# Loading q, k and v as float16 through GpSimd's queue in an attention + Fourier-mixing + FFN kernel

## The chip, the cores and the metric

The kernel runs on one NeuronCore of a Trainium2 chip. A core has TensorE (PE; its weight loads are shown as PEld), VectorE (DVE), ScalarE (ACT), GpSimd (POOL) and SyncE (SP), and 16 DMA engines, which carry what SP, ACT and POOL issue. DMAs issued from SP and ACT are on hardware queues (q1 and q10 in the profile), those from GpSimd on the software queue (q0). The metric is the time of one execution on the device in microseconds, and the median of the runs counts.

## The reference

Inputs are q, k, v of shape (batch 4, heads 8, sequence 768, head size 64), `n_global` 8, `n_local` 96, and two weights w_ch1 (512 x 2048) and w_ch2 (2048 x 512), all float32.

```python
scores = q @ k^T / 8 + bias            # bias = -slope[head] * distance
scores = where(key < 8 or 0 <= row - key < 96, scores, -1e9)
a = softmax(scores)
x = (a @ v)                            # (4, 768, 512), heads side by side
mixed = real(fft(fft(x, axis=1), axis=2))
u = x + mixed
un = (u - mean(u)) / sqrt(var(u) + 1e-6)
out = u + maximum(un @ w_ch1, 0) @ w_ch2
```

## The kernel before

Batches b = 0 to 3 go through attention and mixing one after the other; heads go in pairs, hp = 0 to 3, and n = 4 b + hp numbers the pairs. A batch's 768 rows become three groups of 256 rows for the FFN, c = 3 b + pr, 12 in all.

**Attention.** For each pair, q and k are transposed to head size x sequence (`trans`, tile `qkT`). For b < 2 TensorE does it: 48 transposes of 64x64 into the PSUM tile `pt` (L583), which L594 (DVE) or L598 (ACT) copies out. For b = 2 and 3, SP issues DMA transposes, three a pair (L557, L560). `score` makes the banded scores in three parts g; for b < 2 TensorE also adds the bias (L629, L641) and ScalarE's exponential (L665) writes `ex`; for b >= 2 the exponential goes to `er` (L662) and VectorE multiplies a mask in (L677). `kg_copies` (L544, GpSimd) gathers the 8 global keys; `v_global` and `glob` do the global part, whose exponential is `eg` (L741). `av` multiplies with v (L765, L776) and VectorE divides by the sums (L795, L796), which gives x.

**Mixing.** `bounce` writes x to DRAM and reads it back in another row order (tile `xr`). `fold_s` and `fold_d` (VectorE, some on ScalarE) fold x for the FFT along the sequence, `y_unit` multiplies with a table (L987), `mirror` (GpSimd, L1022 to L1035) reverses columns, `u_unit` does the second FFT (`pu`, L1067), adds x (L1086, L1095), and makes `un` (L1117, L1119). For c < 6 TensorE transposes `un` (`ptu`, L1158), for the others a DMA does. GpSimd makes the inverse deviation (L1133, L1134).

**FFN.** `ph` (L1188) is the first product, for which the first weight must be there; ScalarE or VectorE applies the relu (L1194, L1195). `pg` (L1212, from c = 8 on `pgA` and `pgD`, L1293) is the second product. No `ph` is emitted before the early PSUM banks C and D are given back (token `CD`), that is, before all of b = 0 through `u_unit` and the scores of b = 1.

**Loads.** SP loads q, k and v as float32 into staging tiles, which borrow the space of `hT`, `qs`, `u`, `w1` and `w2` (L407; for v of b >= 2 two half loads, L378). Casts follow: q and k on ACT (L411), DVE (L413) or GpSimd (L415) into the tile `qk`; v for b < 2 on GpSimd (L456) and then through TensorE into its place by products with the identity (`v_place`, L472, with idle products at L465) and out of PSUM by L490 (DVE) and L491 (ACT); v for b >= 2 on GpSimd straight into its place (L501). The weights are loaded and cast by GpSimd's DMAs, eight of 512 KB in float16 (L1472, L1477), after q and k of b = 1. Loads of b = 2 stand behind a small DMA on SP that waits for the last weight (`hold`, L1486, token `gate`).

**Order.** The order of every engine's instructions is written when the program is built, by the class `Plan`. It keeps a clock for each engine, assumes a cost for each instruction and emits what it thinks can start first; `BIAS` moves single ones. Each engine then runs its own list in order, GpSimd's and SP's lists including the DMA issues, and an instruction whose input is late holds those behind it.

Of the kernel before, what the change touches and what calls it, by code (L numbers as in the profile page):

```python
# [22 lines left out]
class Plan:  # L23
# [8 lines left out]
    LAND = {("xw", 0, 0): 34.0, ("xw", 0, 1): 36.0, ("xr", 0): 41.0, ("ld", 4, 2): 47.7, ("ld", 5, 2): 53.4, ("ld", 6, 2): 58.9, ("ld", 7, 2): 64.7, ("w1", 0): 44.6, ("w1", 1): 48.2, ("w1", 2): 52.2, ("w1", 3): 55.8, ("w2", 0): 59.5, ("w2", 1): 63.6, ("w2", 2): 66.6, ("w2", 3): 69.1}  # L32
    LAT = {"ACT": 0.14, "DVE": 0.12, "POOL": 0.08}

    def __init__(self):
        self.t = {"PE": 0.0, "ACT": 0.0, "DVE": 0.0, "POOL": 0.0, "SP": 0.7, "DMA": 1.9, "DMA2": 0.0}
        self.tok = {}
        self.ready = []
        self.pending = []
        self.rings = {}  # L40
        self.left = {}
        self.n = 0
        self.lanes = [0.0] * 8

# [23 lines left out]
    def later(self, ways, needs=(), after=0.0, outs=(), uses=(), ring=None, lat=0.0, dma=0.0, then=None, rank=1, nd=None):  # L68

        self.n += 1  # L70
        if nd is None:
            nd = int(dma > 0 and ways[0][0] in ("SP", "ACT"))
        self.pending.append((self.n, ways, list(needs), after, outs, uses, ring, lat, dma, then, rank, nd))
        self.promote()
# [11 lines left out]
    def first(self):  # L86

        best = None
        for i, (ready, p) in enumerate(self.ready):
            if p[11]:  # L90
                ready = [max(r, self.lanes[p[11] - 1]) for r in ready]
            c = (min(max(self.t[w[0]], r) for w, r in zip(p[1], ready)) - self.AHEAD * (p[10] < 0) + self.BIAS.get(p[4][0] if p[4] else None, 0.0),
# [4 lines left out]

    def emit(self, place):
        ready, (_, ways, needs, after, outs, uses, ring, lat, dma, then, _, nd) = self.ready.pop(place)
        if nd:  # L100
            ready = [max(r, self.lanes[nd - 1]) for r in ready]
# [14 lines left out]
        for _ in range(nd):  # L116
            self.lanes.append(max(end + lat, self.t[eng] + 2.2, *[self.LAND.get(o, 0.0) for o in outs]))
            self.lanes.pop(0)
# [4 lines left out]
        self.promote()  # L123

# [9 lines left out]
    def slot(self, tag):  # L134
# [7 lines left out]
    BIAS = {(1, 5): -0.7, ('ss', 1, 1): -3, (2, 27): -0.7, ('ex', 1, 3, 2): -3, (1, 46): -0.7, ('qk', 10, 1): -1.5, ('c', 't1'): 1.5, ('w1', 2): 3,  # L142
            ('er', 4): -0.7, ('ss', 2, 0): 0.7, ('h', 6, 6): 3, ('qk', 5, 0): 3, ('qkT', 6): -0.7, ('c', 't2'): 0.3, ('ex', 1, 2, 0): -0.7,
            ('xb', 11, 2): -1.5, ('h', 6, 5): 3, ('ss', 2, 1): 0.7, ('qkT', 10): -0.7, ('ex', 0, 2, 1): -1.5, (3, 13): 0.7, (1, 42): 0.7,
            ('un', 7, 0): -0.7, ('s', 11, 3): 0.7, ('x', 0, 3, 2): -1.5, ('qk', 9, 0): 1.5, ('qk', 7, 1): -0.7, ('qk', 0, 0): 1.5,
            ('ld', 15, 1): 1.5, ('h', 5, 1): 0.3, ('h', 5, 4): 0.3, ('qk', 11, 1): 0.7, (3, 73): -1.5, ('un', 0, 1): -1.5, ('y', 1, 2, 0): 3,
            ('er', 2): 0.3, ('qkT', 8): 0.7, ('h', 8, 4): -1.5, ('w1', 0): 3, ('vc', 2): 0.7, (1, 36): 0.3, (3, 47): 0.3, ('ld', 8, 1): -1.5,
            ('ob', 11, 1): -3, ('qkT', 14): 0.7, ('er', 19): -0.3, ('h', 8, 0): -1.5, (1, 92): -0.7, ('kG', 14, 0): 0.3, ('u', 5, 0): 0.3,
            ('w2t', 0): 0.3, ('z', 3, 0): 3, (1, 64): -1.5, ('v', 0, 2, 0): -0.3, ('ss', 6, 1): 3, (2, 21): -1.5, (2, 19): 0.3, ('rd', 10, 0): -0.7,
            ('sid', 2): -0.3, (3, 51): -3, (2, 5): -3}  # L150
    AHEAD = 0.0

    def run(self, streams):

        left = [[(*u, (i, k)) for k, u in enumerate(s)] for i, (s, _) in enumerate(streams)]
        while True:
            best = None
            for i, s in enumerate(left):
                for k, (needs, ring, _, name) in enumerate(s[:self.LOOK if streams[i][1] else 1]):
# [13 lines left out]
                    c = (max(r, self.t["PE"]) + self.BIAS.get(name, 0.0), i, k, g or "", max(r, self.t["PE"]))  # L173
# [37 lines left out]
def kernel(  # L211
# [105 lines left out]
    NBUF = {"hT": 3, "qk": 2, "qs": 3, "qkT": 4, "er": 2, "v0": 2, "eg": 1, "x": 1, "xr": 1, "zy": 1, "eA": 1,  # L317
# [25 lines left out]
    v16 = [kon.tile([P, NS, H, 66], FP16, tag=f"v16{i}", name=f"v16{i}") for i in range(2)]  # L343
# [14 lines left out]
    def vat(n):  # L358

        return ("u", min(n, HP)) if n < HP or n == 2 * HP - 1 else ("qs", 2 + n - HP)  # L360

    def load(b, hp, which):
        n = HP * b + hp
        h0 = 2 * hp
        gate = [("gate",)] if n == FB * HP else []
        if b >= FB:
            srcs = [(0, q), (1, k)] if which == "qk" else [(2, v)]
            for w, src in srcs:
                i = 1 + HP + 3 * (n - FB * HP) + w

                def run(src=src, i=i, w=w):
                    t = stage[("t", n, w)] = buf("qs", i, [P, 2 * NS, Dh], FP32, 1)
                    if w < 2:
                        run_dma(t.rearrange("p (m t) d -> p m (t d)", t=2), src, b, h0)
                        return
                    x = src[b, h0:h0 + 2].rearrange("h s d -> (h s) d").rearrange("(n m t) d -> t m n d", m=64, t=2)
                    for t2 in range(2):
                        nc.sync.dma_start(t[64 * t2:64 * t2 + 64], x[t2])  # L378
                pl.later([("SP", 0.55 if w < 2 else 1.1, run)], free("qs", i) + gate, 0.0, [("ld", n, w)], lat=1.7, dma=1.5 if w < 2 else 2.5, nd=1 + (w > 1))
                if w < 2:  # L380
                    cast_direct(b, hp, w, i)
        elif which == "v":
            def run():
                t = stage[("t", n, 2)] = buf(*vat(n), [P, NS, 2 * Dh], FP32, 1)
                run_dma(t, v, b, h0)
            pl.later([("SP", 0.55, run)], free(*vat(n)) + [("xi",)] * (n >= HP), 0.0, [("ld", n, 2)], lat=1.7, dma=1.45)
        else:
            tag, ti, users, slot = (("hT", hp, 2, 0) if hp < 3 else ("qs", 0, 1, None)) if b == 0 else \
                (("w1", "w2")[hp // 2], 0, 4, 2 * (hp % 2))
            for w, src in enumerate((q, k)):  # L390
                at = (tag, ti) if slot is not None else (tag, w)

                def run(w=w, src=src, at=at):
                    if slot is None:
                        t = buf(at[0], at[1], [P, NS, 2 * Dh], FP32, 1)
                    else:
                        if at not in stage:
                            stage[at] = buf(at[0], at[1], [P, users, NS, 2 * Dh], FP32, users)
                        t = stage[at][:, slot + w]
                    stage[("t", n, w)] = t  # L400
                    run_dma(t, src, b, h0)
                pl.later([("SP", 0.55, run)], free(*at), 0.0, [("ld", n, w)], lat=1.7, dma=1.45)
                cast_qk(b, hp, w, at)

    def run_dma(t, src, b, h0):

        nc.sync.dma_start(t, src[b, h0:h0 + 2].rearrange("h s d -> (h s) d").rearrange("(m p t) d -> p m (t d)", p=P, t=2))  # L407

    def copy_on(on, d, s):
        if on == "ACT":  # L410
            A(d, s, AF.Copy)  # L411
        elif on == "DVE":
            V.tensor_copy(d, s)  # L413
        else:
# [1187 lines left out]
```

The softmax here doesn't subtract the row's maximum and nothing guards it: scores larger than these inputs give would overflow.

## Time and profile before

| | |
|---|---|
| median of 3 runs | 263.72 us (263.44 to 265.83) |
| profiled execution: its time, which is its span | 263.7 us |
| PE, DVE, ACT, POOL busy | 246.5, 173.3, 151.4, 67.2 us |
| packets on q1 (SP), share of the 16 DMA engines | 69,298, 57.3% |
| packets on q0 (GpSimd: the weights), share | 4,224, 9.8% |
| first `ph` product | 53.1 us |
| read from HBM | 31.59 MB |

The page cuts the span into 40 slices of 6.6 us and gives each engine's busy share in tenths. The chain that ended last is followed back from the last instruction, at each step to what released it. A group of instructions is named by its line, engine, operation and tiles. A DMA share of 1.00 means that the packets' times add up to all of the 16 engines' time; it can pass 1, as packets of different queues overlap.

### The profile page before, as it was taken

Reading aid. Unit: us, or ns where it says so; the run is one execution under the profiler, and the core shown is the slowest. Engines: PE = TensorE matmul, PEld = TensorE weight load, DVE = VectorE, ACT = ScalarE, POOL = GpSimd, SP = SyncE. Lnnn points to the kernel's source line nnn. Section 1 sums busy time; section 2 is a strip of 40 time slices with the busy share of each in tenths; the row PEclk is TensorE's granted clock in tenths of the full one; section 3 lists DMA queues with packets and bytes.
Section 4 is the critical chain, followed back from the end, with each engine's and each line's share of the span. In section 5 each row is a group of like instructions: output and inputs, shape, how many; then the busy total and the mean of one; then the engine's idle time right before and its main releaser. Section 6 shows DMA issues by size and latency. Waiting matters only on the chain.

```text
span 263.7 us, 7306 instructions
## 1 busy us (share of the span) xinstructions
PE 246.5 (93%) x3080; PEld 180.6 (68%) x3080; DVE 173.3 (66%) x355; ACT 151.4 (57%) x257; POOL 67.2 (25%) x130
## 2 busy tenths in 40 slices
PE   8678778799999999999999999999999999999993
PEld 2556555578765785776685465677678778888883
DVE  3348999853399536782578958578995935644373
ACT  3276999756647655795682364993544265433300
POOL 1334335980041063514101623011221311000000
PEclk9799999979999999999999999999999999999998
DMA  7999959999699998999999897303641440310222
GB/s 211 296 293 272 309 142 289 225 196 201 125 223 172 283 267 106 183 212 157 218 160 207 205 281 116 90 2 82 145 137 40 23 114 25 83 40 2 80 80 82
DMA packets 76386, 42.02 MB, mean 159 GB/s; under 512 B 33474, under 2 KB 72514, under 8 KB 76354
## 3 DMA queue, kind: packets, MB, share of 16 engines
q1 hardware_dynamic: 69298, 32.65, 57.3%
q0 software_dynamic: 4224, 4.19, 9.8%
q10 hardware_dynamic: 2832, 4.72, 6.8%
q8 instruction: 24, 0.39, 0.6%
q14 instruction: 8, 0.07, 0.1%
HBM read 31.59 MB, written 9.44 MB: 156 GB/s over the span
## 4 chain that ended last, share of the span: by engine, by line
PE 77%; ACT 10%; DVE 5%; DMA 2%; issue 1%; POOL 1%; SPq 1%; DVEq 0%
PE ph L1188 30%; PE pg L1212 21%; PE pgD L1293 5%; ACT ex L665 4%; PE pgA L1293 4%; PE pav L776 4%; PE pu L1067 3%; PE py L987 3%; DMA u<-in_v_dram 2%; PE sc L638 2%; DVE qkT L594 2%; ACT er L662 2%; PE pav L765 1%; ACT un L1117 1%; POOL ww L1035 1%
## 5 line engine op out<-in xcount | busy, mean ns | idle before, releaser
L1188 PE MATMUL ph<-unT,w 128*128 128x256 f16 x768 | 94.7, 276 | 0.0
L1188 PEld LDWEIGHTS <-w 128*128 128x128 f16 x768 | 73.9, 99 | 13.9 <-issue 2.2
L1194 ACT ACTIVATE hT<-ph 128x512 f16<-128x512 f32 x81 | 48.1, 599 | 48.4 <-PE ph L1188 48.3
L1212 PE MATMUL pg<-w,hT 128*128 128x512 f16 x256 | 59.9, 379 | 0.0
L1212 PEld LDWEIGHTS <-hT 128*128 128x128 f16 x256 | 24.3, 98 | 24.7 <-issue 0.6
L662 ACT ACTIVATE er<-sc 128x768 f16<-128x768 f32 (+2 forms) x24 | 21.4, 929 | 6.0 <-PE sc L638 5.9
L665 ACT ACTIVATE ex<-sc 128x992 f16<-128x992 f32 (+2 forms) x24 | 20.6, 937 | 2.1 <-PE sc L641 2.1
L677 DVE TENSOR_TENSOR ex<-er,mk 128x768 f16<-128x768 f16 (+2 forms) x24 | 15.6, 661 | 8.1 <-ACT er L662 7.9
L1133 POOL TENSOR_SCALAR sm<-sm 128x2 f32<-128x2 f32 x12 | 4.4, 368 | 62.8 <-ACT un L1126 62.6
L1221 DVE SCALAR_TENSOR_TENSOR u<-pg,sm,u 128x512 f32<-128x512 f32 x16 | 12.0, 748 | 11.8 <-PE pg L1212 11.8
L1086 DVE SCALAR_TENSOR_TENSOR u<-pu,xr 128x512 f32<-128x512 f32 x18 | 11.7, 688 | 9.0 <-PE pu L1067 9.0
L501 POOL CAST v<-qs 128x768 f16<-128x768 f32 x8 | 6.8, 844 | 40.1 <-DMA qs<-in_v_dram 40.1
L1126 ACT ACTIVATE un<-un 128x512 f16<-128x512 f16 x24 | 15.0, 626 | 3.2 <-DMA unT<-un 1.8
L776 PE MATMUL pav<-v,ex 128*128 128x65 f16 x352 | 16.5, 193 | 0.4 <-ACT ex L665 0.3
L776 PEld LDWEIGHTS <-ex 128*128 128x128 f16 x352 | 15.1, 97 | 2.4 <-issue 1.3
L411 ACT ACTIVATE qk<-qs 128x768 f16<-128x768 f32 x11 | 9.2, 844 | 9.6 <-DMA out_dram<-u 7.0
L1035 POOL COPY ww<-zy 128x512 f16<-128x512 f16 x16 | 9.2, 609 | 21.1 <-PE py L987 17.7
L1195 DVE TENSOR_SCALAR hT<-ph 128x512 f16<-128x512 f32 x15 | 10.3, 688 | 6.1 <-PE ph L1188 6.0
L1117 ACT ACTIVATE un<-u,sm 128x512 f16<-128x512 f32 x13 | 9.2, 720 | 8.7 <-DVE sm L1090 8.5
L1293 PEld LDWEIGHTS <-hT 128*128 128x128 f16 x128 | 12.5, 98 | 1.6
L796 DVE TENSOR_TENSOR x<-pav,rc 128x512 f16<-128x512 f32 (+1 forms) x21 | 12.9, 615 | 0.7
L544 POOL COPY kG<-qkT 64x8 f16<-64x8 f16 x32 | 8.1, 256 | 18.9 <-DVE qkT L594 15.0
(124 smaller groups left out, 382.1 us busy)
## 6 DMA issues: line engine op xcount, KB each, us to landing
out_dram<-u SPq DMA_DIRECT2D x23, 256.0 KB, 2.3
w<-in_moe_w_ch_dram POOLq DMA_DIRECT2D x8, 512.0 KB, 11.2
qs<-in_q_dram SPq DMA_DIRECT2D x9, 384.0 KB, 5.2
qs<-in_k_dram SPq DMA_DIRECT2D x9, 384.0 KB, 5.0
qs<-in_v_dram SPq DMA_DIRECT2D x16, 192.0 KB, 5.0
xr<-xd ACTq DMA_DIRECT2D x3, 768.0 KB, 5.3
u<-in_v_dram SPq DMA_DIRECT2D x5, 384.0 KB, 7.1
w<-in_q_dram SPq DMA_DIRECT2D x4, 384.0 KB, 6.7
```

The costliest lines, as they stand in the source:

```text
L662: A(mine(), cut(pa), AF.Exp, 0.0, 0.125)
L665: A(cut(expst[hp][:, :, g * 512:g * 512 + (384 if g == 2 else 512)]), cut(pa), AF.Exp, 0.0, 0.125)
L677: VT(o, mine(), m, op=ALU.mult)
L776: nc.tensor.matmul(po[:, jj, hh * 65:(hh + 1) * 65], lhsT, v16[b % 2][:, i, h, 0:65], start=(jp == 0 and a == 0), stop=(a == len(ops) - 1) ...
L796: VT(X[b][:, 2 * jp:2 * jp + 2, first * Dh:(first + nh) * Dh].rearrange("p j (h d) -> p j h d", d=Dh), pv[:, :, :, 0:Dh], rc.to_broadcast( ...
L1035: nc.gpsimd.tensor_copy(rev[:, n], T[("y", b)][:, n, :, :, ::-1])
L1126: A(x, x, AF.Square, accum_out=MV[c][:, a, 2:3])
L1188: nc.tensor.matmul(ph[:, a * CH:(a + 1) * CH].rearrange("p (x m) -> p x m", x=2), W1[0][:, d, jb * P:(jb + 1) * P], UNT[c][:, :, d, :], st ...
L1194: pl.later([("ACT", act(512), lambda: A(dst, ph, AF.Relu)), ("DVE", dve(512), lambda: V.tensor_scalar_max(dst, ph, 0.0))], [], e, [("h", c ...
L1212: nc.tensor.matmul(pg, HT[c][:, jb, t * P:(t + 1) * P], W2[0][:, jb, :], start=(jb == 0), stop=(jb == NJ - 1))
L1221: V.scalar_tensor_tensor(UT[c][:, t, :], pg, MV[c][:, t, 3:4], UT[c][:, t, :], op0=ALU.mult, op1=ALU.add)
L1293: nc.tensor.matmul(o, lhs(j), rhs(j), start=(first and j == 0), stop=(j == NK - 1), skip_group_check=True)
```

## The change

All of q, k and v is now loaded by GpSimd's DMAs with float16 destinations, so that the cast happens in the transfer, and no staging tile or cast instruction is left.

- q and k for b < 2: one DMA each a pair and input, 128 partitions x 6 pieces of 512 B read, straight into the tile that TensorE transposes. For b >= 2: four DMAs each, of 64 partitions x 6 pieces of 256 B.
- v for all batches: two DMAs a pair, each of 64 partitions x 12 pieces of 256 B, straight into `v16`, whose layout is now heads before row tiles. `v_place`, `cast_v0` and `cast_v` are gone; a unit of 12 idle products a pair (`idle`) stands where the first two `v_place` had theirs.
- TensorE's transposes for b < 2 are 24 of 64x128 in place of 48 of 64x64, and the result needs no rearranging in its evacuation. DMA transposes for b >= 2 are two a pair in place of three.
- Order of the loads on GpSimd's queue: q, k and v of b = 0, q and k of b = 1, w1; then GpSimd copies a cell of b = 0's `xr`, so that what stands behind it waits for the row read of x; then v of b = 1, w2, and the loads of b = 2 and 3. `hold` is gone. The tables t1 and t2 are issued after x's writes.
- `qk` has four buffers (two before), `qs` and `v0` none; `u` is no longer lent to v. GpSimd's memsets move behind its first loads. The planner's costs, biases and lanes for GpSimd's DMAs are new, so the order changes on every engine.

```diff
-    v16 = [kon.tile([P, NS, H, 66], FP16, tag=f"v16{i}", name=f"v16{i}") for i in range(2)]
+    v16 = [kon.tile([P, H, NS, 66], FP16, tag=f"v16{i}", name=f"v16{i}") for i in range(2)]
...
     def load(b, hp, which):
         n = HP * b + hp
         h0 = 2 * hp
...
+        if which == "v":
+            for t in range(2):
+                def run(t=t):
+                    nc.gpsimd.dma_start(v16[b % 2][64 * t:64 * t + 64, h0:h0 + 2, :, 0:Dh].rearrange("m h i d -> m (h i) d"),
+                                        v[b, h0:h0 + 2].rearrange("h (i m t) d -> t m (h i) d", m=64, t=2)[t])
+                pl.later([("POOL", 0.84, run)], ([("avdone", b - 2)] if b > 1 else []) + order_needs(b, "v"), 0.0, [("v", b, hp, t)],
+                         lat=2.2, dma=0.63, rank=order_rank(b, hp, "v"))
+            return
+        tag, ti = ("hT", n // 2) if n < 6 else ("qk", n - 6)
+        for w, src in enumerate((q, k)):
+            if b >= FB:
+                for x in range(4):
+                    def run(w=w, src=src, t=x // 2, h=x % 2):
...
+                        nc.gpsimd.dma_start(qk16[n][64 * t:64 * t + 64, w, :, h], src[b, h0 + h].rearrange("(i m t) d -> t m i d", m=64, t=2)[t])
...
+                nc.gpsimd.dma_start(qk16[n][:, w].rearrange("p h n t d -> p (h n) (t d)"),
+                                    src[b, h0:h0 + 2].rearrange("h s d -> (h s) d").rearrange("(m p t) d -> p m (t d)", p=P, t=2))
...
+    def order_needs(b, which):
+        return [("wl", 7)] if b > 1 else [("wgate",)] if b == 1 and pl.ORD[which, 1] > pl.ORD["gate"] else []
...
+    def idle(b, hp):
+        n = HP * b + hp
...
+            for _ in range(12):
+                nc.tensor.matmul(pv[:, 1, 0:P], EG[:, 0:P], EG[:, 0:P], start=True, stop=True)
...
-                        for a in range(2):
-                            for h in range(2):
-                                r = slice(64 * a, 64 * a + 64)
-                                nc.tensor.transpose(o[64 * h:64 * h + 64, a, w, x, t], src[r, w, x, t, h], idn[r, r],
-                                                    tile_position=(64 * a, 64 * h))
+                        for h in range(2):
+                            nc.tensor.transpose(o[64 * h:64 * h + 64, w, x, t], src[:, w, h, x, t], idn,
+                                                tile_position=(0, 64 * h))
...
-            needs = [("qk", 7, 1), ("free", "w1", 0)] if i == 0 else [("wl", 3), ("free", "w2", 0)] if i == 4 else [("wl", i - 1)]
+            needs = ([("qk", 7, 1, "i")] if i == 0 else [("wl", i - 1)]) + [("wgate",)] * (i == 4)
...
-        pl.later([("SP", 0.45, hold)], [("w2", 3)], 0.0, [("gate",)], nd=1)
+        cell = kon.tile([1, 2], FP16, tag="cell", name="cell")
+        pl.later([("POOL", 0.2, lambda: nc.gpsimd.tensor_copy(cell, XR[0][0:1, 0, 0:2]))], [("xr", 0), ("wl", 3)], 0.0, [("wgate",)], rank=pl.ORD["gate"])
```

## The prediction, as put on record before the run

> **What bounds the kernel now.** I read the page's totals and slices first, then busy time by stage, the chain that ended last, and the DMA queues by stage.
>
> ```profile
> PE 246.5 (93%) x3080; PEld 180.6 (68%) x3080; DVE 173.3 (66%) x355; ACT 151.4 (57%) x257; POOL 67.2 (25%) x130
> PE   8678778799999999999999999999999999999993
> DMA  7999959999699998999999897303641440310222
> ```
>
> From slice 9 on (about 53 us) TensorE is full and stays so. The stages, whose columns are the busy us of each engine, the granted clock, the DMA share and GB/s:
>
> ```profile
> 25.00:53.00 28.00, 21.76 (x588) 15.56 (x587) 26.00 (x60) 25.63 (x42) 15.10 (x29) 1.00 1.01 245
> 53.00:76.00 23.00, 23.00 (x325) 18.49 (x314) 10.82 (x23) 12.93 (x30) 7.75 (x13) 0.93 1.05 185
> 76.00:160.00 84.00, 83.47 (x808) 55.50 (x807) 58.25 (x111) 53.80 (x85) 24.41 (x44) 1.00 1.06 203
> ```
>
> Before 53 us VectorE (26.0 of 28) and ScalarE (25.6 of 28) are full and TensorE waits; afterwards TensorE is the bound. The chain (start, us, what) shows the hand-over:
>
> ```profile
> 35.94 2.59 ACT ex L665 x3
> 38.53 0.60 ACT zy L855 x2
> 39.13 3.85 ACT ex L665 x5
> 42.99 0.52 ACT eg L741
> 43.51 1.74 ACT ex L665 x2
> ...
> 51.78 0.38 ACT v L491
> 52.16 0.62 ACT un L1117
> 52.78 0.04 issue
> 52.82 0.32 PE ptu L1158 x16
> 53.14 1.06 PE ph L1188 x7
> ```
>
> So time = start of the first `ph` (53.1) + 210.6 us of TensorE work. The DMA engines are full too until 70 us. First the stage 6 to 30 us, then 52 to 70, then the end of that stretch on SP's queue:
>
> ```profile
> DMA packets 13737, 6.94 MB, mean 289 GB/s; under 512 B 357, under 2 KB 13723, under 8 KB 13732
> ...
> DMA packets 3336, 3.26 MB, mean 181 GB/s; under 512 B 106, under 2 KB 3334, under 8 KB 3334
> ...
> SPq L1486 <- DMA w<-in_moe_w_ch_dram: 27.2, 1, 27.2
> ```
>
> The second stage is the w2 load. L1486 waits for it until 69.8 us, and the first `pg` products (L1212, at 64.9) need its first quarter.
>
> **What the skill says.** "DMA: Bandwidth & Descriptors", section "SWDGE vs HWDGE vs iDMA": a cast in a DMA can only be issued from GpSimd. The trace agrees as far as it goes: the w loads cast and are GpSimd's. Same page, "Specifications": full rate needs 512 B pieces. Here 256 B loads of v (72 to 74 us) run at 325 GB/s, against 289 for 512 B ones, so the trace does not show this for 256 B; no run shows 128 B writes. "SBUF — State Buffer", section "SBUF: two separate sides": some VectorE modes lock GpSimd out of writing descriptors. The w issues at 39.3 us, with VectorE full, took 0.74 and 0.95 us against a median of 0.755, so little of that shows.
>
> **Removed.** Casts of q and k (L411, L413, L415), of v (L456, L501), and the placing of v for b < 2 (L472, L490, L491). In 25 to 53 us ScalarE loses the `qk` casts at 29.44, 30.81 (two) and 34.74: 0.84+1.56+0.85 = 3.25 us, and L491 at 51.8: 0.5, so 3.75 us after `eg` at 28.7. VectorE loses two L490 of 0.56 = 1.1 us there and had 2.0 us idle. All of these except the idle lie on engines that set the start of `ph`. After 53 us TensorE loses three L472 units (60 of 96 products lie before; 12 take 0.36 us), so 1.1 us on the bound.
>
> **Transposes.** 48 of 64x64 took 0.57 us. The 24 new ones stream 128 columns; the plain products here show 128x256 at 0.87/8 = 0.109 us, so 128 columns cost 0.054: 24 x 0.054 = 1.3 us if one by one, 0.65 if the two column halves overlap as the old ones did. I take 0.65; the high end adds 0.7 us at each of three chain pieces (2.1). The evacuation L594 keeps its 0.95 us. The 24 idle products stay 24 in number, no longer behind a cast of v.
>
> **First arrival.** Now scores begin at 11.4 us and the first exponential at 12.48, because the v placement with its idle products (9.3 to 11.5) stands before them. Without it: q and k issue by 2.6 us, where SP's are out by 1.8, so k lands near 6.3 instead of 5.4; transpose 0.65, evacuation 0.95, score to exponential 1.1 as now: first exponential near 9. These 3.5 us are not all kept, as the next step shows.
>
> **GpSimd's queue.** A w issue makes 512 packets in 0.755 us. A load of 768 packets therefore costs 0.755 (if only the instruction counts) to 1.13 (if packets do); I take 0.94. In the changed order the second `kG` half that `glob` of heads 4 to 7 needs stands behind 15 q/k loads, 8 v halves and the first w1 load: 24 x 0.94 = 22.6, plus memsets 1.0, `kG` halves 7 x 0.22 = 1.5, start 0.7: 25.8 us; ends 21.3 and 30.4. With `pgl` 0.6 this puts `eg` at 26.5 instead of 28.7: 2.2 us earlier. ScalarE then gains 2.2+3.75 = 5.9, VectorE 2.2+1.1+2.0 of idle = 5.3. **The smaller counts: first `ph` at 47.8.**
>
> **DMA up to w2.** Per engine a 512 B load has 48 packets: 6.94 MB at 289 GB/s is 28 ns each, 1.34 us. A w load is 9.8% x 263.7/8 = 3.2 us. Before: 24 x 1.34 + 8 x 3.2 + about 12 for constants, x's round trip, start and receipt = 70, as seen. After: 16 q/k loads and 16 v halves of 768 smaller packets. The w stream reads 512 B per 3.2/32/4 = 25 ns; so a q/k packet is 25 to 28, a v packet (256 B) 13 (325 GB/s) to 28. I take 26 and 16: 16 x 1.25 + 16 x 0.77 + 25.6 + 12 = 70. So w2 ends near 70 again, while TensorE wants its last quarter at first `ph` + 20.6 = 68.4: 1.0 to 1.6 us of new waiting, I take 1.0. The gate (GpSimd reads x's row, then v of b = 1, then w2) stands behind the mirror copies, now over at 49.4, then 44; eight v issues of 0.94 and two L1134 pairs end at 54: w2's last quarter cannot land before 54+4 x 3.2+2 = 69 either.
>
> **Later loads.** For b = 2 and 3, 64 q/k issues of 384 packets: 0.38 to 0.57 us each, and 32 v halves in all. GpSimd is busy 24.4 of 84 us from 76 to 160; it gets 64 x 0.5 = 32 us and loses 12 us of casts (L501 6.8, L415 5.7): 44 of 84. Behind these issues queue `kG`, the mirror copies and L1133/L1134. The first b = 2 scores (now 105.6) come 49 us after first `ph` = 97; their loads start behind v of b = 3, which waits for av of b = 1 (62): 62+8 x 0.94 = 70, mirror copies 3.5, eleven issues 5.5, landing 3, two transposes of 4.5 in turn = 91. Cover 6 us; nothing added. SP loses its loads and 8 of 24 transposes.
>
> **Sum.** 263.7 - 5.3 - 1.1 + 1.0 = **258.3 us**. The profiled span, 263.7, is the median of the runs, so nothing is added.
>
> **Rivals.** (a) As above: 258.3 (256 to 260.5); chance 0.42. (b) GpSimd's issue cost is near 0.755 and packets near 25 and 13 ns: w2's DMA sum falls by 16 x 0.05 + 16 x 0.15 = 3.2 us, by 3.3 more if slice 6, half idle, fills: 63.5. `eg` at 22 allows a first `ph` of 43.5, which wants w2 at 64.1: no wait, 263.7-9.6-1.1 = 253. For it, the 3.5 us won at the start; against, VectorE has no idle left for more: chance 0.2. (c) GpSimd's queue holds `kG` to 30.4: `eg` at 31, first `ph` at 53.1+2.3-3.1 = 52, w2 later by as much: 262 to 264; chance 0.15. (d) **Slower:** small casting packets carry a fixed cost. If each takes 13 ns more than plain (41 and 29 ns), DMA up to w2 is 16 x 1.97 + 16 x 1.39 + 37.6 = 91 us; `pg` stands until then, with 210.6-1.1-20.6 = 189 us of TensorE's work left: 280; half that surcharge gives 270. It decides from w2 landing later than 74.8 (68.4 plus the 6.4 gained elsewhere): 4.8 us, or 3.1 ns on each of an engine's 1536 packets. For it: these stages have no DMA idle at all; against: w's rate. Chance 0.23, about half of it between 264 and 270. That the change does nothing is not a case: nearly every load is rewritten.
>
> **Numbers.** Faster than 1% (261.1) holds (a) and (b): 0.62. Within 1%, which is about what a measurement tells from no change: (c): 0.14. Slower: (d) and the end of (c): 0.24. Range 252 to 270: below is 0.05, above about 0.13. All one distribution; (a)'s own range is 256 to 260.5.
>
> **What would show it.** First `ph` at 46 to 50; first `ex` near 9; GpSimd issues near 0.94; the load of w2 over near 70 and a short TensorE gap before the second `pg` group; TensorE full afterwards. Wrong if q0's packets of 128 B average over 20 ns, if `eg` waits on `kG` after 29 us, or if TensorE idles before the first b = 2 score.

## The result, and the profile after

The changed kernel takes 264.23 us (median of 20 runs, 262.37 to 266.92) against 264.03 us for the kernel before on the same chip (20 runs). The ratio is 0.9989 with a 95% interval of 0.9966 to 1.0012: no measurable change. 258.3 us was forecast. The profiled execution has a span of 263.4 us, from the first instruction to the last; the measured time of the same execution is 265.2.

The page's totals and slices, as shown for the kernel before:

```profile
PE 245.1 (93%) x2784; PEld 179.8 (68%) x2784; DVE 165.0 (63%) x341; ACT 136.4 (52%) x234; POOL 120.5 (46%) x216
PE   7878966699999999989999999999999999999994
POOL 8989332997475999989941151101001311000000
DMA  8999999699999999999999947202540331311122
```

VectorE and ScalarE were relieved (173 to 165 us, 151 to 136), and GpSimd nearly doubled (67 to 120). Now the stages (busy us of PE, PEld, DVE, ACT, POOL; clock; DMA share; GB/s):

```profile
25.00:53.00 28.00, 20.56 (x436) 15.02 (x434) 21.04 (x52) 20.73 (x35) 13.78 (x28) 1.00 1.17 198
53.00:76.00 23.00, 22.74 (x292) 18.30 (x285) 14.82 (x29) 13.79 (x31) 15.82 (x24) 0.93 1.47 156
76.00:160.00 84.00, 82.78 (x828) 55.76 (x827) 55.84 (x110) 44.56 (x72) 60.10 (x106) 1.00 1.30 151
```

Before 53 us, VectorE and ScalarE have 7 us of slack each, where they had 2.0 and 2.4, and still TensorE does not start `ph` earlier. The chain that ended last (start, us, what) says what it waits for:

```profile
31.13 0.58 SPq L713
31.75 10.62 DMA xd<-x
42.45 6.09 DMA xr<-xd
48.63 0.71 DVE u L993 x2
...
52.77 0.43 PE ptu L1056 x13
53.20 3.33 PE ph L1086 x16
```

It is x's round trip through DRAM (`bounce`, now L713 and L721). x's last write is issued at 31.1 us, 2.4 us earlier than the 33.5 of before, but the row is back at 48.5, where it was back at 42: 17.4 us for 8.5. VectorE, which adds the row in `u`, waits for it for only 1.5 us (its waits between 25 and 53 us):

```profile
DVE u L993 <- DMA xr<-xd: 1.5, 1, 1.5
```

`u` also needs what comes of the folds (products with a table, copies, second-FFT products). The last of those copies on VectorE ended at 47.2 us, 1.4 us before the row was back; in the kernel before it ended at 47.5. So a second chain, "the folds" from here on, stands close behind the row, and it has hardly moved. The DMA queues between 28 and 50 us (packets, MB, share of the 16 engines; then KB each and median us from issue to landing) name the neighbour:

```profile
q0 software_dynamic: 2983, 2.29, 66.1%
q1 hardware_dynamic: 2032, 2.36, 36.5%
...
xr<-xd SPq DMA_DIRECT2D x1, 768.0 KB, 6.1
xd<-x SPq DMA_DIRECT2D x2, 192.0 KB, 9.5
t<-t2m SPq DMA_DIRECT2D x1, 384.0 KB, 12.2
```

In the kernel before, the weights' packets began at 43 us, when the row was back. Now the four w1 loads are issued from 23.4 to 27.0 us and are on the engines until 47.3, beside x's writes and their reading. The Trainium skill's page "DMA: Bandwidth & Descriptors", section "Queues, rings and completion order", says that an engine alternates between the queues that have work, a packet at a time; the trace agrees as far as the sharing goes: x's two last writes took 3.2 us before and 9.5 now (medians to landing). That the turns are single packets, no run here shows.

A second place lies at 115 us. The chain there, and the only wait of TensorE between 85 and 160 us (us in total, times, longest):

```profile
89.80 10.49 POOL qk L401 x16
...
109.47 3.02 DMA qk<-in_q_dram
...
113.44 5.96 DMA qkT<-qk
119.45 0.38 PE sc L542 x4
```

```profile
PE sc L542 <- DMA qkT<-qk: 1.2, 2, 0.9
```

b = 2's scores wait for q and k that GpSimd issues one after another from 80 us on. GpSimd's groups of issues (instructions, busy us, mean ns of one, idle before):

```profile
L389 POOL DMA_DIRECT2D v<-in_v_dram x32 | 24.4, 787 | 5.3 <-PE pav L674 2.1 <-DMA w<-in_moe_w_ch_dram 1.5 <-issue 1.1
L401 POOL DMA_DIRECT2D qk<-in_k_dram x32 | 22.1, 777 | 0.2
L401 POOL DMA_DIRECT2D qk<-in_q_dram x32 | 22.1, 748 | 1.0 <-DMA v<-in_v_dram 0.9
L409 POOL DMA_DIRECT2D hT<-in_q_dram x6 | 5.3, 891 | 0.8 <-POOLq L1472 0.8
```

A load of 384 pieces costs nearly what one of 768 does. A third place is a detour of the chain over ScalarE, 2.8 us at 70.6 to 73.4, where a relu stands behind ScalarE's own two issues of x's write. TensorE has other products there and stands still for 0.26 us only.

### The profile page after: what moved, and what is told of

The parts are those of the page before. It is cut to its first block, busy times and chain, and to the rows that moved or that the text cites. A ratio compares the mean times of both kernels' runs of the same rounds, so it can differ in the third digit from the quotient of the medians.

```text
span 263.4 us, 6686 instructions
## 1 busy us (share of the span) xinstructions
PE 245.1 (93%) x2784; PEld 179.8 (68%) x2784; DVE 165.0 (63%) x341; ACT 136.4 (52%) x234; POOL 120.5 (46%) x216
## 4 chain that ended last, share of the span: by engine, by line
PE 66%; DMA 15%; POOL 12%; ACT 2%; DVE 2%; issue 1%; ACTq 1%; SPq 1%; DVEq 0%; POOLq 0%
PE ph L1086 26%; PE pg L1110 16%; POOL qk L401 7%; PE pgD L1191 5%; DMA xd<-x 4%; PE pgA L1191 4%; PE pav L674 3%; PE py L885 3%; DMA qk<-in_k_dram 3%; DMA xr<-xd 2%; DMA qkT<-qk 2%; DMA hT<-in_k_dram 2%; PE sc L542 2%; PE pu L965 2%; POOL ww L933 2%; POOL hT L409 1%
## 5 line engine op out<-in xcount | busy, mean ns | idle before, releaser
L1092 ACT ACTIVATE hT<-ph 128x512 f16<-128x512 f32 x82 | 48.4, 598 | 53.4 <-PE ph L1086 51.7
L1110 PE MATMUL pg<-w,hT 128*128 128x512 f16 x256 | 61.2, 379 | 0.0
L1110 PEld LDWEIGHTS <-hT 128*128 128x128 f16 x256 | 24.4, 98 | 22.8 <-issue 0.4
L389 POOL DMA_DIRECT2D v<-in_v_dram x32 | 24.4, 787 | 5.3 <-PE pav L674 2.1
L567 ACT ACTIVATE er<-sc 128x992 f16<-128x992 f32 (+2 forms) x24 | 21.5, 927 | 6.6 <-PE sc L542 5.3
L1031 POOL TENSOR_SCALAR sm<-sm 128x2 f32<-128x2 f32 x12 | 2.6, 216 | 48.7 <-ACT un L1024 48.2
L582 DVE TENSOR_TENSOR ex<-er,mk 128x992 f16<-128x992 f16 (+2 forms) x24 | 15.0, 628 | 15.1 <-ACT er L567 15.0
L401 POOL DMA_DIRECT2D qk<-in_q_dram x32 | 22.1, 748 | 1.0 <-DMA v<-in_v_dram 0.9
L401 POOL DMA_DIRECT2D qk<-in_k_dram x32 | 22.1, 777 | 0.2
L933 POOL COPY ww<-zy 128x512 f16<-128x512 f16 x16 | 9.4, 616 | 25.3 <-PE py L885 18.6
L1024 ACT ACTIVATE un<-un 128x512 f16<-128x512 f16 x24 | 14.8, 618 | 6.5 <-PE ptu L1056 4.5
L900 ACT ACTIVATE zy<-py 128x512 f16<-128x512 f32 (+1 forms) x12 | 9.4, 812 | 12.9 <-PE py L885 6.6
L501 DVE COPY qkT<-pt 128x1536 f16<-128x1536 f16 x7 | 6.7, 956 | 12.0 <-PE pt L494 12.0
```

Source lines behind the costliest of these rows:

```text
L389: nc.gpsimd.dma_start(v16[b % 2][64 * t:64 * t + 64, h0:h0 + 2, :, 0:Dh].rearrange("m h i d -> m (h i) d"), v[b, h0:h0 + 2].rearrange("h ( ...
L401: nc.gpsimd.dma_start(qk16[n][64 * t:64 * t + 64, w, :, h], src[b, h0 + h].rearrange("(i m t) d -> t m i d", m=64, t=2)[t])
L567: A(mine(), cut(pa), AF.Exp, 0.0, 0.125)
L582: VT(o, mine(), m, op=ALU.mult)
L933: nc.gpsimd.tensor_copy(rev[:, n], T[("y", b)][:, n, :, :, ::-1])
L1024: A(x, x, AF.Square, accum_out=MV[c][:, a, 2:3])
```

## The experiments

The theories: **T1**, x's round trip, held by the w1 stream in the same engines, sets the first `ph`; **T5** adds the folds on VectorE as a second chain that ends with it, behind b = 1's last k load (T1' is one of the two alone: the row, but in the expectation for the k load ahead of w1 below, the folds). **T2**, ScalarE, VectorE or `kG` set it. **T3**, what the DMA engines must carry up to w2 pins the time, whatever the first `ph`. **T4**, losses behind the start: ScalarE's issue, and GpSimd's issues for b = 2. All edits are to the changed kernel; ratios are to the kernel before, measured beside each run on the same chip, with 95% intervals.

### One edit each, the order written anew

`Plan` rewrites every engine's list when a need is changed, so these runs carry a new order with them.

The tables t1 and t2 ahead of x's writes in SP's list:

```diff
-dma_const(t1_sb..., t1_d, 1.2, ("c", "t1"), [("xwi", 0, 0)])
+dma_const(t1_sb..., t1_d, 1.2, ("c", "t1"))
-dma_const(t2_sb..., t2_d, 1.2, ("c", "t2"), [("xwi", 0, 1)])
+dma_const(t2_sb..., t2_d, 1.2, ("c", "t2"))
```

> From the changed kernel, the two loads of constants t (0.4 MB each) that stand between x's writes in SP's queue go ahead of them; the first w1 quarter stays where it was. In the changed kernel x's last write is issued at 31.1 us, its row is back at 48.5 and the first ph runs at 53.2. (T1) x's round trip through DRAM sets the first ph, and SP's queue and its transfers hold it: the row is back 1 to 4 us earlier, first ph 49.5 to 52, time 261 to 263.5. If the w1 stream on GpSimd's queue is the larger part of the delay, less than 1.5 us is won. (T2) ScalarE, VectorE or the key sums on GpSimd set the first ph: it stays at 53 +- 0.3 although the row is back earlier; 264. (T3) the loads of v and w2 behind the gate pin the time: first ph earlier, but TensorE waits before the pg products by as much; 264.

Measured: 274.28 us, ratio 1.0364 (1.0294 to 1.0434). In the first 25 us GpSimd's queue moved 13,328 packets, 15,962 without the edit, and TensorE is busy for 17.7 us, for 19.8 without it; x's row is back only at 52.6 (48.2), first `ph` at 58.9. All three expectations missed the cost at the front, where the 0.8 MB of tables now stand among the first loads. How much of the 3.6% is that, and how much the new order, this run does not show.

One w1 quarter, or none, ahead of x's row:

```diff
-needs = ([("qk", 7, 1, "i")] if i == 0 else [("wl", i - 1)]) + [("wgate",)] * (i == 4)
+needs = ([("qk", 7, 1, "i")] if i == 0 else [("wl", i - 1)]) + [("wgate",)] * (i == 1)
-[("xr", 0), ("wl", 3)], 0.0, [("wgate",)], rank=pl.ORD["gate"])
+[("xr", 0), ("wl", 0)], 0.0, [("wgate",)], rank=pl.ORD["gate"])
```

For none, `i == 0` and the need of `wl` away; v of b = 1 also waits for the last w1 issue in both.

> From the changed kernel, only the first quarter of w1 is issued before x's row is back; the gate opens on the row alone, and the other three quarters of w1, then v of b = 1, then w2 follow it. (T1) the w1 stream is what stretched x's round trip from 8.5 to 17.4 us: the row is back at 40 to 43, first ph at 46 to 48.5 (engines: 47.8). The time is 258 to 261 if w2 comes in time. (T2) first ph stays near 53: 264 or more. (T3) first ph goes to about 48, but three w1 quarters (9.6 us) now lie behind the gate that opens 7 us earlier, so w2 lands 2 to 3 us later than in the changed kernel (near 75), and TensorE waits for w1 and w2 by as much as it won: 263 to 267.

> From the changed kernel, all of w1 is issued behind x's row. (T1) x's round trip is alone with the loads of q and k of b = 1 and is as in the kernel before, 8.5 to 9.5 us: the row is back at 39.5 to 41. But the first w1 quarter lands no earlier than row + 1 + 3.2 + 2 = 46 to 47, so first ph is 46.5 to 48.5 and waits for w1. (T2) the row returns early and first ph stays near 53. (T3) whatever the first ph, the DMA engines stand half idle while the row is on its way (9 us), and w2 lands 5 to 6 us later than in the changed kernel: TensorE waits before pg, time 266 to 269.

Measured: 273.9 us for one quarter ahead (runs from 268.3 to 274.7, too wide for a ratio; the profile is that of the longest) and 273.27 us for none, ratio 1.0289 (1.0235 to 1.0342). The row's last packet came at 43.1 and 38.5 us (48.2 in the changed kernel). With less of w1 beside it the row is earlier, as T1 has it. But the gate copy ran only at 51.3 and 46.3 us, since the planner had put it behind the mirror copies (L933) in GpSimd's list, and the rest of w1 stood behind the gate: first `ph` 55.6 and 53.4. The times lie above T3's too (263 to 267 and 266 to 269), so none of the three had them; which part is order and which is DMA is open here.

x of b = 1 on SP's queue in place of ScalarE's:

```diff
-on, eng = ("ACT", nc.scalar) if b else ("SP", nc.sync)
+on, eng = ("ACT", nc.scalar) if b > 1 else ("SP", nc.sync)
```

> From the changed kernel, x of b = 1 goes through DRAM on SP's queue instead of ScalarE's. (T4) the 2.8 us without matrix products at 70.6 to 73.4 us, in which ScalarE's relu stands behind ScalarE's own two issues of x's write (0.15 + 1.35 us), is a loss of its own: it shrinks to about 1 us and the time falls by 1 to 2 us, 262 to 263. (T3) w2's landing near 72 would have held the pg products anyway: the gap turns into a wait for w2 of the same length, 264 +- 0.7. First ph unchanged at 53.2 in both.

Measured: 265.02 us, ratio 0.9993 (0.9964 to 1.0022). The chain has no ScalarE piece at 70 us any more:

```profile
69.53 1.75 PE ph L1086 x16
71.27 0.86 PE pg L1110 x4
72.13 1.75 PE ph L1086 x16
73.88 5.18 PE pg L1110 x24
```

ScalarE's detour was no wait for w2, and it is gone, but no time is won. The expectation took it for 2.8 us without products; TensorE had lacked work there for 0.26 us, so there was next to nothing to win, and the chain goes on to GpSimd's issues for b = 2 as before.

The k load of b = 1 that stood behind the first w1 quarter, ahead of it; then with w1 split around the row and the gate early in GpSimd's list:

```diff
-needs = ([("qk", 7, 1, "i")] if i == 0
+needs = ([("qk", n, w, "i") for n in range(4, 8) for w in range(2)] if i == 0
```

```diff
-('wgate', '*', 0): 3
+('wgate', '*', 0): -8, ('w1', '*', 2): -8, ('w1', '*', 3): -8
```

> From the changed kernel, the one k load of b = 1 that is issued behind the first w1 quarter (24.67 us, landed near 36.7) goes ahead of it; everything of w1 stays ahead of x's row. (T5) two chains end together near 48.5 in the changed kernel: x's row, and the folds, which stand in VectorE's order behind the copy L501 of the transposes of that k load. This run shortens the second alone by the 3.1 us of one w1 quarter: the copy L501 that was at 36.9 comes at 33 to 34, but u still waits for x's row near 48.5 and first ph stays at 53 +- 0.5; 263 to 265. (T1') the folds alone are the chain and the row is beside them: first ph falls to 50, time 260.5 to 261.5. (T2) nothing moves, the copy L501 neither.

> As the run with all of w1 behind x's row (row back near 38, first u 44.9, gate held on GpSimd behind the mirror copies to 46.3, first ph 53.4), but the gate and the four w1 issues stand before the mirror copies in GpSimd's order. (T5) with both chains shortened and the gate out of the mirror copies' way, w1 is issued from 38 us, its first quarter lands near 43, the last near 53; first u at 45, first ph at 49 to 50. w2's last quarter then lands at 71 to 73 against 70 wanted, so that 1 to 2 us of the gain go again: time 260 to 262.5. (T3) what the DMA engines move up to w2 pins the time: first ph earlier, but the gap before pg grows by as much or more, since they idled while the row was on its way; 264 to 268. (T2) first ph stays near 53; 264 or more.

> From the changed kernel: the last k load of b = 1 ahead of w1, two quarters of w1 ahead of x's row and two behind it, and the gate ahead of the mirror copies in GpSimd's order. (T5) the row has 6.4 us of w1 less beside it than in the changed kernel: back at 42 to 44.5, first u 45 to 46, first ph 49.5 to 50.5; the DMA engines have work throughout and w2 lands at 68 to 70, in time: 259.5 to 261.5, the best of the four. (T3) w2 no earlier than now, since the sum of bytes is the same: 263 to 265 with a gap of 3 to 4 us before pg.

> As the run before it with one quarter of w1 ahead of x's row and three behind it. (T5) row back at 40 to 41, first u 45, first ph 49 to 50, w2 at 69 to 71: 259.5 to 262. (T3) 263 to 266. If all three split runs have a first ph near 50 and times within 1 us of the kernel before, the start of ph is not what sets the time any more and something behind it is (w2, or the issues of b = 2's q and k on GpSimd).

| run | time us | ratio | row back | first `ph` | w2's last piece |
|---|---|---|---|---|---|
| changed kernel | 264.23 | 0.9989 | 48.2 | 53.1 | 71.3 |
| k before w1 | 268.64 | 1.0163 (1.0101 to 1.0225) | 45.9 | 51.0 | 70.1 |
| w1 after the row | 268.22 | 1.0152 (1.0096 to 1.0207) | 37.8 | 50.4 | 71.7 |
| two quarters before | 271.9 | 1.0242 (1.0166 to 1.0318) | 43.6 | 56.8 | 72.6 |
| one quarter before | 272.33 | 1.0294 (1.0242 to 1.0346) | 40.6 | 53.3 | 74.2 |

The first `ph` can be moved. VectorE's and ScalarE's lists are new here too, so this alone does not put T2 out (r6 below does, with their lists kept). And yet both runs with an earlier `ph` are slower. In the first of them TensorE stands still near 110 us (waits from 85 to 125 us):

```profile
PE sc L542 <- DMA qkT<-qk: 4.9, 1, 4.9
```

It arrives earlier at b = 2's scores, and these come no earlier. So half the issues for b = 2 and 3, alone and with the k edit. The rows of q and k then stand in another order than the mask's, so the results of b = 2 and 3 are others, with all the work still done. The second pair of runs halves the issues of q alone, whose rows the products can read with a stride of two, and computes everything:

```diff
-for x in range(4):
+for x in range(2):
...
-nc.gpsimd.dma_start(qk16[n][64 * t:64 * t + 64, w, :, h], src[b, h0 + h].rearrange("(i m t) d -> t m i d", m=64, t=2)[t])
+nc.gpsimd.dma_start(qk16[n][:, w, :, h], src[b, h0 + h].rearrange("(i p) d -> p i d", p=P))
```

> From the changed kernel, q and k of b = 2 and 3 are loaded by two DMAs of 128 partitions for each tensor and head pair instead of four of 64: the same bytes and the same 128-byte pieces, half the issues (32 for 64). Their rows then stand in natural order while the mask of the scores keeps even-odd order, so the results of b = 2 and 3 are others; no work is left out. (T4) GpSimd's issuing, 0.65 to 0.75 us for each 384-piece load, is a second wall behind the first ph: with issues of 768 pieces at 0.75 to 0.89 us GpSimd's busy time from 76 to 160 us falls from 60 to 44 us, the b = 2 scores no longer wait for the transposed q and k at 115 to 120 us (1.1 us of matrix work lost there), 262 to 263.5. (T3) the lost 1.1 us comes back elsewhere: 264 +- 0.5. First ph stays at 53.

> The halved issues of the run before together with the k load of b = 1 ahead of the first w1 quarter. That edit alone moved the first ph from 53.2 to 51.0 and yet made 268.6, with 7 us of TensorE's work missing from 110 to 120 us, where b = 2's scores wait for q and k whose issues follow each other on GpSimd from 87 to 107 us. (T4) that queue is the wall which the earlier start runs into: with half the issues the hole is gone and the start is kept: 259.5 to 262. (T3, or an order written by the planner that is bad for another reason) the hole stays whatever the issues cost: 266 to 269.

> From the changed kernel, only q of b = 2 and 3 is loaded by 128 partitions (two DMAs for four); its rows stand in natural order and the scores and the far-key products read q's columns with a stride of two, so everything is computed as in the reference. 48 issues for 64. (T4) two thirds to a half of what halving both brings: 262.5 to 264. If the strided reads of q cost TensorE time, the score products take more than 263 ns each and the gain is lost.

> The k load of b = 1 ahead of w1, with q of b = 2 and 3 by 128 partitions, everything computed. (T4) 16 issues fewer give about 10 us of GpSimd's time back over 80 to 135 us, of which some 4 to 5 lie ahead of b = 2's last q and k: the hole at 110 to 120 us shrinks from 7 to 2 or 3 us: 262 to 265. (T3) 266 to 269 as without it.

Measured: 267.72, 273.02, 271.02 and 272.78 us; ratios 1.0119 (1.004 to 1.0198), 1.0229 (1.0133 to 1.0325), 1.027 (1.0188 to 1.0352) and 1.0347 (1.0259 to 1.0435). In the first, GpSimd's issues of q and k for b = 2 and 3 fell from 44 to 27 us and the wait of b = 2's scores from 1.2 to 0.7, but a new hole opened where there was none (waits of TensorE, 155 to 180 us):

```profile
PE sc L542 <- DVE u L984: 1.4, 1, 1.4
PE sc L542 <- ACT er L567: 1.0, 1, 1.0
```

None of these waits is for a load; the order of TensorE's list is another one. Of the runs with a new order, all but the one with x on SP's queue came out slower than the kernel before, those with a ratio by 1 to 4%, so the edit and the order cannot be told apart in them. From here on the edits are made where an instruction is emitted, so that the planner writes the same plan.

### The order kept

In the next four runs the lists of TensorE, VectorE, ScalarE and SyncE are those of the changed kernel, instruction for instruction; only GpSimd's differs. r1 holds the first w1 issue back until the k load is out. r5 does the same and also emits the gate and w1's last two quarters ahead of the mirror copies. r2 leaves every second q and k issue of b >= 2 empty and lets the other carry both (the results of b = 2 and 3 are others again, no work is left out):

```diff
-nc.gpsimd.dma_start(qk16[n][64 * t:64 * t + 64, w, :, h], src[b, h0 + h].rearrange("(i m t) d -> t m i d", m=64, t=2)[t])
+if t == 1:
+    nc.gpsimd.dma_start(qk16[n][:, w, :, h], src[b, h0 + h].rearrange("(i p) d -> p i d", p=P))
```

r4 is r5 and r2 together.

> From the changed kernel, only two DMA issues change places on GpSimd: the last k load of b = 1 goes ahead of the first quarter of w1. The order of every other engine is kept. (T5) VectorE's copy L501 of that k's transposes, at 36.9, comes 3 us earlier, the folds behind it too, and first ph falls from 53.2 to 51 to 51.7, where x's row holds it. The time falls by less, since b = 2's scores near 115 us wait for GpSimd's issues: 262 to 263.5. (T1') x's row alone is the chain: first ph stays at 53, 264. (T3) first ph earlier and w2 in the way: 264.

> As r1, and the last two quarters of w1 and the gate go right behind the reading of x's row on GpSimd, ahead of the mirror copies; the order of every other engine is kept. (T5) 6.4 us of w1 less beside the row: back at 42.5 to 44.5 (48.5 in the changed kernel), first ph at 49 to 50.5. v of b = 1 still follows the mirror copies, w2 lands at 68 to 71. Time 259.5 to 262.5, the upper end if GpSimd's issues hold b = 2's scores. (T3) w2 late by what was won: 263 to 265. (T2) first ph near 53.

> From the changed kernel, each second issue of b = 2's and 3's q and k is left away and the other moves both halves (128 partitions, 768 pieces of 128 bytes; their rows then stand in natural order while the mask keeps even-odd order, so results of b = 2 and 3 are others, no work is left out). The order of every other engine is kept. (T4) GpSimd's 60.1 busy us in 76 to 160 fall to about 44, the 1.1 us of matrix work missing at 115 to 120 come back: 262.3 to 263.3. (T3, or the issues hidden) 264 +- 0.4.

> The edits of r5 and of r2 together, order of every other engine kept (rows of b = 2's and 3's q and k in natural order, as in r2). (T5 and T4) the two walls stand one behind the other, so together they give what both give alone or more: first ph 49 to 50.5 and no hole at 115 us, 258.5 to 261. (T3) 263 or more.

The last pair computes everything as the reference does. r7 is r1 with only q of b = 2 and 3 in halved issues (48 for 64); the scores and the far-key products read q's columns with a stride, and full blocks:

```diff
-TT[n][lo:lo + 64, 0, i * P:i * P + cw], start=True, stop=True)
+TT[n][lo:lo + 64, 0, i * P:i * P + cb].rearrange("p (j m t) -> p j t m", t=2, m=64), start=True, stop=True)
```

r6 is r7 with w1's last two quarters (2 and 3 in the code) behind v of b = 1 and ahead of w2; gate and mirror copies stay where they were:

```diff
 def wload(i):
+    if i in (2, 3) and not late:
+        return
+    if i == 4:
+        late.append(1)
+        wload(2)
+        wload(3)
```

> From the changed kernel: the last k load of b = 1 ahead of w1, the last two quarters of w1 behind v of b = 1 (gate and mirror copies where they were), and q of b = 2 and 3 in two issues of 128 partitions, read with a stride by the products. All is computed; VectorE, ScalarE and SyncE keep their order. (T5) x's row is back at 43 to 44, the mirror copies run at 43.5 to 47, first u at 45, first ph at 50.5 to 51.5. (T3) The DMA engines have half of w1, v of b = 1 and w2 left from 47 us, 6 x 3.2 + 8 x 0.72 = 25 us, so w2's last quarter lands near 73 against 71.5 wanted: 1 to 2 us of the start's gain are lost there. Time 260.5 to 262.5. If the first ph is at 51 and the time is not below that of r7, w2's landing is the third wall.

> As r6 without the split: k ahead of w1, and q of b = 2 and 3 in half the issues; order of the other engines kept, all computed. First ph at 52.5 to 53.2 as with the k load alone; (T4) 16 issues fewer give back about half of what halving both did: 0.995 x 0.995 of the kernel before, 262 to 263.5. The strided, 256 wide score products cost some 0.3 us.

| run | time us | ratio | row back | first `ph` | span - first `ph` | w1's 3rd quarter | w2's last piece |
|---|---|---|---|---|---|---|---|
| changed kernel | 264.23 | 0.9989 (0.9966 to 1.0012) | 48.2 | 53.1 | 210.3 | 41.9 | 71.3 |
| r1 | 263.84 | 0.9948 (0.9923 to 0.9972) | 48.4 | 53.2 | 209.3 | 42.0 | 71.1 |
| r5 | 266.04 | 1.0036 (1.0000 to 1.0072) | 43.1 | 54.8 | 209.5 | 48.6 | 73.0 |
| r2 | 261.62 | 0.9889 (0.9855 to 0.9922) | 47.7 | 52.5 | 207.5 | 41.0 | 70.8 |
| r4 | 264.34 | 0.9985 (0.9957 to 1.0012) | 42.6 | 54.3 | 207.4 | 48.2 | 71.6 |
| r7 | 262.15 | 0.9898 (0.9868 to 0.9928) | 47.2 | 52.6 | 207.7 | 41.6 | 70.9 |
| r6 | 266.24 | 1.0057 (1.0027 to 1.0086) | 42.8 | 49.7 | 214.1 | 59.2 | 73.2 |

**GpSimd's issues.** TensorE's wait for `qkT` between 85 and 160 us, 1.2 us in the changed kernel and 1.3 in r1, is not there any more in r2, and the time falls. By how much depends on the pair: r2's ratio of 0.9889 against the changed kernel's 0.9989 is 1.0%, or 2.6 us, but these two were not measured together. Of the pairs that were, r4 against r5 differs in this edit alone and gives 0.5% (1.3 us; the intervals just overlap), r2 against r1 0.6%. So halving the issues is worth some 1.3 to 2.6 us, and the wait at 115 us is about 1.2 of it. The profiles say the same: the three runs with halved issues need 207.4 to 207.7 us from the first `ph` on, r1 and r5 209.3 and 209.5. (The changed kernel's 210.3 is not quite comparable: from 53 to 76 us its granted clock was 0.93, in the others 0.97 to 1.00, and 0.07 of 23 us is 1.6 us.) In r2 TensorE is full from 76 to 160 us, and GpSimd has 48 busy us for 60:

```profile
76.00:160.00 84.00, 84.00 (x835) 56.45 (x833) 54.40 (x109) 43.76 (x73) 48.30 (x75) 1.00 1.29 157
```

**The k load.** In r1 the load landed 3.6 us earlier (32.6 us for 36.1), but the copy L501 that was to follow it stayed where it was (37.05 us for 36.74), because the two copies ahead of it in VectorE's list ran 1.0 and 1.7 us later; x's row and the first `ph` stayed too. So r1 did not shorten the folds and says nothing against T5. (In r7, which has the same edit, that copy ran at 35.26 us and the folds ended at 45.7 for 47.2.) Other runs decide it. In r5 and r6, and in the two runs above with none of w1 ahead of the row (e2 and g1, with new orders), the row landed anywhere from 38.0 to 43.4 us, and the first `u` ran at 44.7 to 45.3 in all four. In r6 it waits for the folds' last product, not for the row (between 45 and 76 us):

```profile
DVE u L1001 <- PE pu L973: 0.2, 1, 0.2
```

So T5 holds: the row ends last, the folds end 1.4 us before it, and the row alone can win no more than VectorE's 1.5 us of waiting. r1's ratio is 0.4% below the changed kernel's; the two intervals overlap and were not measured together, so nothing is built on it.

**x's row.** r5 brought it back 5 us earlier and lost it at once on GpSimd. Its waits between 40 and 56 us:

```profile
POOL cell L390 <- DMA xr<-xd: 7.1, 1, 7.1
...
PE pu L981 <- POOL rev L937: 3.9, 1, 3.9
```

The gate waits for the row, and the mirror copies, which the `pu` products need, wait behind the gate. r6 takes that away, and against r7 it differs in the place of two w1 quarters only: the row is back 4.4 us earlier and the first `ph` runs 2.9 us earlier, at 49.7, where the folds hold it. So x's round trip beside the w1 stream held the first `ph`, and T2, with VectorE's and ScalarE's lists kept, is out as the only cause. But the time is 4 us longer, and its chain and waits (45 to 76 us) say why:

```profile
44.48 0.75 PE pu L973 x10
45.25 0.71 DVE u L1001 x2
...
52.42 0.79 POOL v L391
...
54.24 5.39 DMA w<-in_moe_w_ch_dram
59.68 4.07 PE ph L1094 x24
```

```profile
PE ph L1094 <- DMA w<-in_moe_w_ch_dram: 4.6, 1, 4.6
```

The quarter that was out of the row's way landed at 59.2 in place of 41.6, and w2 at 73.2 in place of 70.9. TensorE is busy for 18.4 of the 23 us from 53 to 76, where r7 fills them. It waits for w1, not for w2, and w1 is late because GpSimd issues it late, at 54.2 us: the gate copy runs at 45.9, behind the mirror copies, and the eight v issues come first. The DMA engines had room meanwhile. Between 38 and 46 us (40 slices, r6 above r7) they moved 0.97 MB in r6 and 2.16 in r7:

```profile
DMA  4436210039029958999685300001001000000000
```

```profile
DMA  9999999999999999999999999999999999997973
```

So T3 is right that in r6 the earlier first `ph` is paid for at the weights, but there GpSimd's list, not the DMA engines' work, sets the price. An order that gives the row its way and w1 its time was not found; whether there is one stays open.

**A better version.** r7 is faster than both kernels, by 1.02% (0.72 to 1.32) than the one before, and computes everything.

**The order's own price.** Three edits were run both ways, with the order written anew and with it kept: the k load (1.0163 and 0.9948), all issues halved (1.0119 and 0.9889), and the k load with q's issues halved (1.0347 and 0.9898, r7). The new order made each of them 2.2 to 4.5% slower.

## Why the prediction was wrong, step by step

**Removed casts: right in kind.** Between 25 and 53 us VectorE was busy for 5.0 us less and ScalarE for 4.9. Part of VectorE's is work that now stands later: from 53 to 76 us it has 14.8 busy us for 10.8.

**First arrival: half right.** The first exponential came at 11.48 us, 1.0 us earlier than before; near 9 was forecast. k landed at 8.1 for 6.3: its issue was over at 3.1 us for 2.6, and then it took 5.0 us, where the plain load of before took 3.7. And the 12 idle products still stand ahead of the scores, from 9.06 to 10.45.

**GpSimd's queue up to `kG`: right.** `eg` of heads 4 to 7 ran at 26.17 us (26.5 forecast). The 768-piece issues took 0.74 to 0.89 us, 0.94 was assumed.

**"The smaller counts: first `ph` at 47.8": this is the step that failed.** It took ScalarE, VectorE and, before them, `kG` as the only walls of the first `ph`, since the chain of before ran through them, and booked what these engines were spared as time won. Two things that it gave no time stand there. x's round trip was not on that chain; it was counted among "about 12" us of DMA work only. But the change moved w1 from behind the row to ahead of it, in the same engines, and the round trip doubled to 17.4 us and became the chain. And the folds stand in VectorE's list behind the copy for b = 1's last k load, which the change put behind the first w1 quarter; it landed at 36.1 us, where before the last was in at 33.0. So the folds ended at 47.2 us for 47.5, although VectorE had 7 us of slack (at 45.7 in r7, with that load ahead of w1). r6, with that load ahead of w1 and the row back early, has its first `ph` at 49.7: 3.4 of the 5.3 us that were missing. The last 1.9 us stay open; no run came to 47.8.

**The DMA sum up to w2: right in size, and its wait wrong.** w2's last piece came at 71.3 us (70 forecast). The 1.0 us of waiting set for it was not seen: the only wait of TensorE there was 0.26 us, for a relu.

**Later loads, "cover 6 us; nothing added": wrong, a mis-sized term.** 64 issues took 44.2 us, 32 were forecast from 0.5 us each; they measure 0.75 to 0.78. Busy time of GpSimd from 76 to 160 us is 60.1 us, 44 forecast. The forecast worked out its cover for b = 2's first scores, and there it held: they began at 105.3 us and waited for nothing (the forecast has 105.6 for the kernel before, whose trace has 108.1). The pairs after them waited, from 115 to 120 us, 1.2 us in all, and halving the issues brought 1.3 to 2.6 us. An earlier first `ph` can lose more here: with the k load ahead of w1 and a new order the same wait was 4.9 us.

**Sum.** From the first `ph` to the end 210.3 us were measured and 210.5 forecast, by other terms: three `pvp` units fewer, no wait for w2, and the scores' wait. The profiled span, 263.4, is 5.1 us above the forecast: 5.3 were lost ahead of the first `ph`, at 53.1 for 47.8, and 0.2 won behind it. The forecast took span and time to be the same, as the table of the kernel before does; in the runs on record the time is 1.7 to 2.7 us longer, which changes none of the differences above.

**The rivals.** (c) came nearest, with 262 to 264, by luck: its reason, `kG` held to 30.4 us, did not occur. (d) fell: a packet of q or k cost an engine 23.6 ns, and where v's were most of them, one cost 14.9 (below), no surcharge. (b) had the packets about right, but its first `ph` of 43.5 passes over the same two chains.

## What to carry to other kernels

The chain that ended last names one wall; before a relief is booked, the other chains that could end there are to be priced with their new neighbours. Here two of them ended 1.4 us apart, so clearing one alone could show little. A store and reload through DRAM costs what the other queues let it have at that moment. Moving a stream behind such a round trip frees the trip, but the stream then waits for its issuer: in r6 the DMA engines stood nearly still from 43 to 46 us while loads waited in GpSimd's list. And where an order is written by a planner, an experiment must keep that order, or its re-planning (2.2 to 4.5% in three edits here) is measured along with the edit.

## What the runs showed of the hardware

Casting packets overlap in an engine. From 6 to 12 us the changed kernel's queues held nothing but q and k:

```profile
q0 software_dynamic: 4072, 1.02, 174.1%
```

4,072 packets in 6 us on 16 engines is one per 23.6 ns, while a packet's own time is 41 ns (a share of 174%). From 12.5 to 16.5 us 4,290 packets (share 221.7%) pass at one per 14.9 ns; 3,626 of them are v's, with 32 ns of their own, and 573 still q's and k's. A hardware queue beside them suffers: reading the row took 4.3 us with no software packets beside it (r6), 6.1 and 6.2 us with w1 beside it (the changed kernel, r7). The kernel before moved 512 B without a cast at 28 ns. The Trainium skill's page "DMA: Bandwidth & Descriptors", section "Specifications", asks for 512 B for full rate. In bytes read, this mix of mostly 256 B pieces runs at about 305 GB/s (3,626 x 256 B and 573 x 512 B in 4 us, an estimate), against 289 for the plain 512 B loads of before, so little of that rule is seen here; in bytes written, half as many, it is about 153.

The issue of a load on GpSimd is mostly a fixed cost: 0.75 to 0.78 us on average for 384 pieces and 0.79 to 0.89 for 768.
